# Attention with a routed expert layer: q, k and v remainders of two head pairs in one operation, and the last keys' unit ahead of the first bank

## The chip, the cores and the metric

The kernel runs on one core of a Trainium2 chip. The core has TensorE (PE, matrix products into PSUM), VectorE (DVE), ScalarE (ACT) and GpSimd (POOL) for elementwise work, and DMA queues, most of which are started here by SyncE (SP). Each engine takes its instructions in the order in which the program issued them, and waits where data is not there yet. The metric is the time of one launch on the device, in microseconds (us). The profile is one further execution, taken by the hardware profiler; its span is the stretch from its first instruction to its last.

## The reference

```
cum = np.cumsum(np.maximum(s, 0.0), axis=-1)
bias = -(cum[:, :, :, None] - cum[:, :, None, :])
scores = np.where(causal, -1000000000.0, q @ k.T / 8 + np.minimum(bias, 0.0))
attn = softmax(scores) ; x = attn @ v          # 8 batches, 8 heads, 576 positions, width 64
logits = x @ w_gate                            # 4608 tokens of width 512, 8 experts
...                                            # (token, expert) pairs in order of their logit, 576 tokens for each expert
out[mask] = np.maximum(x[mask] @ w1[e], 0.0) @ w2[e]
```

Causal attention with a bias that falls with a running sum, then a layer of eight experts of which each token gets one. The choice depends on the order of all logits, so the kernel keeps about float32 accuracy: it splits float32 values into a 16-bit part and a 16-bit remainder and multiplies both.

## The kernel before, in words

The change touches attention alone. Attention runs over 16 **groups** g of four heads: two pairs of heads (`pr` 0 and 1), each of two heads (`par` 0 and 1). An order written by hand (`run`, line 600) cuts each group into 14 **units**, seven for each pair of heads. In each unit it issues one unit of scores of the group, then what was posted for that unit, then what the plan `T` puts there for other groups: loads, splits, the maxima, the products with v of scores made seven units earlier.

- **Split of q, k and v** (`prep_units` line 212, `vprep_units` line 271). A raw tile holds both pairs of heads, 2 x 576 elements a partition. `hi2` (line 262) writes the 16-bit part on ACT; `lo2` (line 265) the remainder, x times scale minus the 16-bit part, on DVE, one operation for each pair of heads: for q, k and v six operations of 128x576 a group, all on line 267. After each, `pop` runs a queued small DVE step (denominators). The plan's entries `LO=(2, 3, 5, 7)` and `VLO=(13, 11)` give the units, counted from the start of the split. The split of q and k is made three groups ahead; five copies on SP (`b1a` to `b3`) then bring the parts to their partitions.
- **Maxima** (`spass_units`, line 284). PE makes scores into PSUM and DVE takes their maxima (line 297). `m1` (line 343) scales the nine maxima on POOL in three small steps (lines 350 to 352). They come back to Q through a transpose and two small DMAs (`m2`, `m3`).
- **Scores** (`st_units`, line 374). For each pair of heads there are six **banks** of 512 columns (three for each `par`), and one unit `last` of 128 columns for the last 64 keys. `fin` (line 389) writes P = exp(scores) in float32 on ACT (line 391) and posts the **remainder R** = P minus its upper 16 bits (line 393) three units later: bank (0, 0) and `last` on DVE, the other five on POOL. The entry `RD=((0, 0),)` names the banks whose R is on DVE. For the very last group it is `RE`, in which bank (0, 0) of the second pair of heads is not named, so that it goes to POOL there.
- **Products with v** (`pv_units`, line 438). PE multiplies P's upper half with v and its remainder, and R with v (lines 457 to 459), from the seventh unit on behind the scores. The banks' columns of P and R follow the 128 columns of `last` (`P0 = 128`). The tile of the last 64 queries is the one that needs `last`.
- Around it POOL also writes the remainder of the result (line 496), and SP the result and its transposes to be used for the logits.

After attention the router sorts and assigns the tokens, and the experts run with weights that POOL gathers.

Of the kernel before, what the change touches and what calls it, by code (L numbers as in the profile page):

```python
# [8 lines left out]
F32 = mybir.dt.float32  # L9
F16 = mybir.dt.float16  # L10
BF = mybir.dt.bfloat16
I32 = mybir.dt.int32
AF = mybir.ActivationFunctionType
OP = mybir.AluOpType
# [13 lines left out]
YS = 8.0 * QS * QS  # L28
# [7 lines left out]
LA = 2  # L36
GS = 64.0
START = ((None, None, -25, 4), (None, None, -5, 7), (-13, 0, 10, 6), (3, 7, 21, 5))
T = dict(HI=(0, 1, 2, 2), LO=(2, 3, 5, 7), B=(3, 5, 8, 8, 10), VHI=(6, 8), VLO=(13, 11), RD=((0, 0),), RT=(3, 3),
         XH=(23, 27, 24), XL=(26, 29, 34), XT=(27, 29, 30, 30, 36), LG=(33, 34, 38, 43, 45), M=(2, 5, 10), G=(-50,  # L40
         -42, -26), V=(-17, -14), PV=(7, 7), NT=(1, 1), NA=(1, 1, 1, 0), RE=(((0, 0),
         (0, 2), (1, 1)), ((0, 1),)), NE=(0, 0, 0, 0), RP=1, RQ=204, TL=((16, 23), (16, 23)))
# [4 lines left out]
P0 = 128  # L47
PW = 1536
# [3 lines left out]
def strided_hi(ap):  # L52
    return ap.bitcast(BF).rearrange("p (c two) -> p c two", two=2)[:, :, 1]


class Attention:
# [155 lines left out]
    def prep_units(self, g):  # L212
# [8 lines left out]
        def b1a(odd=True, x="qk"):  # L221
            if odd:
                if "q" in x:
                    d(q_(0, 0, 1), q_(64, 1, 0))
                if "k" in x:
                    d(K[0:64, 0, 1], K[64:128, 1, 1])
            else:
                d(q_(0, 0, 0), q_(0, 1, 0))
                d(K[0:64, 0, 0], K[0:64, 1, 1])
# [20 lines left out]
        if g < 2:  # L250
            b0 = [lambda o=o, x=x: nc.scalar.activation(o, x[0:64], AF.Copy, scale=QS)
                  for o, x in ((q_(0, 0, 0), q), (K[0:64, 0, 0], k))]
            if g:
# [4 lines left out]
            return hi, lo, b0, b1a, b1b, b2, b3  # L258
        return (list(zip(T["HI"], hi)) + list(zip(T["LO"], lo)) +
                list(zip(T["B"], (lambda: b1a(False), b1a, b3, b1b, b2))))  # L260

# [1 line left out]
        return [lambda p=p: self.nc.scalar.activation(o[:, p], x[:, p], AF.Copy, scale=sc) for p in range(2)]  # L263

    def lo2(self, x, h, o, sc):
        def f(p):
            self.nc.vector.scalar_tensor_tensor(o[:, p], x[:, p], sc, h[:, p], op0=OP.mult, op1=OP.subtract)  # L267
            self.pop()
        return [lambda p=p: f(p) for p in range(2)]

    def vprep_units(self, g):
        st = self.st[g]
# [3 lines left out]
        return ([(0, lambda: self.nc.gpsimd.memset(V[:, :, :, 64:65], 1.0))] +  # L276
                list(zip(T["VHI"], self.hi2(st["rv"], V[:, :, :, 0:64], VS))) +
                list(zip(T["VLO"], self.lo2(st["rv"], V[:, :, :, 0:64], Vl, VS))))

# [94 lines left out]
    def st_units(self, g):  # L374

        nc, st = self.nc, self.st[g]
        Q, K = st["Q"], st["K"]
        units = []

        def mm(ps, c0, n, par, pr, ki, q0, diag=False):  # L380
            ks = slice(128 * ki, 128 * ki + 128)
            nc.tensor.matmul(ps[:, c0:c0 + n], K[0:70, 0, par, pr, ks], Q[0:70, 0, pr, par, q0:q0 + n],  # L382
                             start=True, stop=False)
            nc.tensor.matmul(ps[:, c0:c0 + n], K[:, 1, par, pr, ks], Q[:, 1, pr, par, q0:q0 + n],  # L384
                             start=False, stop=not diag)
            if diag:
                nc.tensor.matmul(ps[:, c0:c0 + 128], self.identb, self.mT, start=False, stop=True)

        def fin(ps, pr, c0, n, gp):
            P, R = st["P", pr], st["R", pr]  # L390
            nc.scalar.activation(P[:, c0:c0 + n], ps[:, :n], AF.Exp, scale=1.0 / YS)  # L391
            eng = nc.gpsimd if gp else nc.vector
            self.post(lambda: eng.tensor_tensor(R[:, c0:c0 + n], P[:, c0:c0 + n], strided_hi(P)[:, c0:c0 + n],  # L393
                                                op=OP.subtract), T["RT"][0 if gp else 1])

        def bank(pr, par, j):
            if par == 0 and j == 0:
                st["P", pr] = self.w.tile([128, P0 + 2 * PW], F32, name="P")
                st["R", pr] = self.w.tile([128, P0 + 2 * PW], F16, name="R")
            ps = self.ps_t.tile([128, 512], F32, name="pst")  # L400
            o, t = 64 * par, 0 if par else 512
            if j == 0:
                mm(ps, 0, 512, par, pr, 0, o, diag=True)
            elif j == 1:
                mm(ps, 0, 64, par, pr, 0, t)
                for ki, c0, n in ((1, 64, 384),):
                    mm(ps, c0, n, par, pr, ki, o + 128, diag=True)
                mm(ps, 448, 64, par, pr, 1, t)
            else:
                mm(ps, 0, 256, par, pr, 2, o + 256, diag=True)  # L410
                mm(ps, 256, 64, par, pr, 2, t)
                mm(ps, 320, 64, par, pr, 3, t)
                mm(ps, 384, 128, par, pr, 3, o + 384, diag=True)
            fin(ps, pr, P0 + par * PW + 512 * j, 512, (par, j) not in
                (T["RE"][pr] if g == 2 * self.nb - 1 else T["RD"]))

        def last(pr):


            ps = self.ps_t.tile([128, 512], F32, name="pst")  # L420
            nc.tensor.matmul(ps[:, 0:128], self.identb, self.mL, start=True, stop=False)
            for par in range(2):
                q0 = self.q0(par, 4)
                for a, n in ((0, 70), (1, 128)):
                    k0 = (2 * par + pr) * S + 512 - 64 * par
                    nc.tensor.matmul(ps[:, 64 * par:64 * par + 64],
                                     K[0:n, a].rearrange("p h r s -> p (h r s)")[:, k0:k0 + 128],
                                     Q[0:n, a, pr, par, q0:q0 + 64], start=False, stop=(par == a == 1))
            fin(ps, pr, 0, 128, False)

        for pr in range(2):
            for par in range(2):
                for j in range(3):
                    units.append(lambda pr=pr, par=par, j=j: bank(pr, par, j))
            units.append(lambda pr=pr: last(pr))
        return units

    def pv_units(self, g, pr):
# [980 lines left out]
```

## Time and profile before

| what | us |
|---|---|
| median of 3 runs (859.68 to 864.87) | 862.95 |
| the profiled execution, its own time | 858.84 |
| its span | 857.1 |
| attention in it, to about | 336 |
| a group of attention in the middle (14 units) | 18.65 |
| PE, DVE, ACT, POOL busy over the span | 761.5, 613.0, 387.0, 478.4 |

How to read it: the shares over the span mix two parts. Up to about 336 us the core works on attention, after it on the router and the experts, which the change does not touch. Numbers of the whole page therefore say little of the change; the rows by stage do. The profile names an operation by its line, its engine and its tiles (out<-in), so `R<-P` is the remainder of the exponentials on line 393, on POOL or on DVE. The granted clock of TensorE over the span is 0.942 of full speed, and 1.00 in most of attention. A duration includes the time in which an operation that was issued could not get on.

### The profile page before, as it was taken

How to read it: one execution, taken by the hardware profiler on the slowest of the kernel's cores; microseconds unless marked ns; L12 is line 12 of the kernel's file. 1: busy time of each engine (PE TensorE's matmuls, PEld its weight loads, DVE VectorE, ACT ScalarE, POOL GpSimd, SP SyncE). 2: the span in 40 equal slices, each digit the busy share in tenths (PEclk: the TensorE clock that was granted, in tenths of full speed). 3: DMA queues.
4: the chain of work that ended last, by engine and by line, in shares of the span. 5: the costliest groups of instructions: out<-in, count | busy, mean ns of one | idle time of the engine just before them, and what ended most of it. 6: DMA issues, size and time to landing. Idle time of an engine off the chain costs nothing.

```text
span 857.1 us, 22612 instructions
## 1 busy us (share of the span) xinstructions
PE 761.5 (89%) x9241; PEld 482.7 (56%) x9241; DVE 613.0 (72%) x1578; ACT 387.0 (45%) x866; POOL 478.4 (56%) x587
## 2 busy tenths in 40 slices
PE   8887899989889998269989999998989969959996
PEld 3576777877777787147545455454444525424442
DVE  6789999999999978668768878776677737115110
ACT  5466778878768787024213333231232113214110
POOL 5577899999989996062353534633462342432101
PEclk9689999999999999589999999999998979969999
DMA  6865999898988806052393837546283290491001
GB/s 176 249 178 151 198 238 236 207 236 234 232 205 223 177 31 141 33 187 67 114 188 103 223 101 194 151 134 169 81 211 107 95 221 28 125 210 62 31 13 43
DMA packets 122222, 128.69 MB, mean 150 GB/s; under 512 B 79781, under 2 KB 88329, under 8 KB 122118
## 3 DMA queue, kind: packets, MB, share of 16 engines
q1 hardware_dynamic: 103938, 74.31, 37.1%
q0 software_dynamic: 15744, 52.46, 20.3%
q8 instruction: 72, 1.18, 0.6%
q10 hardware_dynamic: 2436, 0.48, 0.3%
q14 instruction: 32, 0.26, 0.1%
HBM read 71.99 MB, written 19.49 MB: 107 GB/s over the span
## 4 chain that ended last, share of the span: by engine, by line
PE 48%; DVE 24%; issue 12%; DMA 5%; POOL 5%; ACT 3%; another core or an unknown queue 1%; ACTq 0%; SPq 0%; POOLq 0%; DVEq 0%
PE py L1146 15%; PE ph L1109 15%; DVE mr L297 7%; DVE R L393 3%; PE pht L1113 2%; PE py L1137 2%; DVE K L267 2%; DVE Vl L267 2%; PE ph L1111 2%; PE cnt L883 2%; POOL R L393 2%; PE pi L1013 1%; DVE Q L267 1%; DMA md<-mt 1%; DMA Q<-Q 1%
## 5 line engine op out<-in xcount | busy, mean ns | idle before, releaser
L393 POOL TENSOR_TENSOR R<-P 128x512 f16<-128x512 f32 x158 | 195.9, 1254 | 19.3 <-ACT P L391 19.3
L1109 PE MATMUL ph<-xT,w1p 128*128 128x512 f16 x696 | 187.1, 391 | 11.8 <-issue 11.7
L1146 PE MATMUL py<-w2p,hT 128*128 128x512 f16 x768 | 177.1, 381 | 0.3 <-issue 0.3
L1051 POOL DMA_INDIRECT wst<-in_w_dram,iw x96 | 98.3, 1024 | 138.8 <-DVE iw L857 40.4
L1113 PE MATMUL pht<-xT,w1p 128*128 128x64 f16 x768 | 139.0, 195 | 8.9 <-issue 8.7
L297 DVE TENSOR_REDUCE mr<-pss 128x1 f32<-128x512 f32 (+4 forms) x224 | 133.5, 608 | 9.9 <-PE pss L305 5.7
L391 ACT ACTIVATE P<-pst 128x512 f32<-128x512 f32 (+1 forms) x224 | 120.5, 563 | 41.4 <-PE pst L384 14.6
L1158 POOL DMA_INDIRECT out_dram<-y,ids x40 | 42.7, 1068 | 155.9 <-ACT y L1148 127.2
L1109 PEld LDWEIGHTS <-w1p 128*128 128x128 f16 x696 | 69.5, 100 | 93.8 <-issue 22.5
L1146 PEld LDWEIGHTS <-hT 128*128 128x128 f16 x768 | 70.2, 98 | 81.5 <-issue 5.4
L1117 ACT ACTIVATE hT<-ph 128x512 f16<-128x512 f32 x64 | 38.1, 597 | 169.5 <-PE ph L1109 89.0
L459 PE MATMUL po<-V,R 128*128 128x65 f16 x960 | 112.9, 195 | 1.3 <-POOL R L393 1.0
L457 PE MATMUL po<-V,P 128*128 128x65 f16 x960 | 112.4, 196 | 0.9 <-DVE xf L479 0.9
L458 PE MATMUL po<-Vl,P 128*128 128x64 f16 x960 | 112.3, 194 | 0.0
L382 PE MATMUL pst<-Q,K 70*128 70x64 f16 (+4 forms) x512 | 104.7, 253 | 4.3 <-ACT P L391 3.0
L384 PE MATMUL pst<-Q,K 128*128 128x64 f16 (+4 forms) x512 | 105.4, 253 | 0.0
L1126 DVE SCALAR_TENSOR_TENSOR hT<-ph,hT 128x512 f16<-128x512 f32 x64 | 43.8, 687 | 84.9 <-ACT hT L1117 54.4
L457 PEld LDWEIGHTS <-P 128*128 128x128 bf16 x960 | 91.1, 99 | 5.6 <-issue 0.2
L303 PE MATMUL pss<-K,Q 67*128 67x512 f16 (+3 forms) x256 | 72.5, 311 | 22.8 <-DVE mr L297 19.6
L459 PEld LDWEIGHTS <-R 128*128 128x128 f16 x960 | 90.3, 98 | 1.8 <-POOL R L393 1.5
L458 PEld LDWEIGHTS <-P 128*128 128x128 bf16 x960 | 90.2, 100 | 1.1 <-issue 1.0
L1113 PEld LDWEIGHTS <-w1p 128*128 128x128 f16 x768 | 71.3, 99 | 12.9 <-issue 12.2
(223 smaller groups left out, 1562.7 us busy)
## 6 DMA issues: line engine op xcount, KB each, us to landing
rq<-in_q_dram SPq DMA_DIRECT2D x32, 288.0 KB
rk<-in_k_dram SPq DMA_DIRECT2D x32, 288.0 KB
rv<-in_v_dram SPq DMA_DIRECT2D x32, 288.0 KB
Q<-Q SPq DMA_DIRECT2D x62, 144.0 KB
K<-K SPq DMA_DIRECT2D x62, 144.0 KB
xs<-xp SPq DMA_DIRECT2D x32, 256.0 KB
wst<-in_w_dram,iw POOLq DMA_INDIRECT x96
xs<-xp SPq DMA_DIRECT2D x8, 128.0 KB
```

Source lines behind the costliest of these rows:

```text
L297: nc.vector.tensor_reduce(o, ps, AX.X, OP.max)
L382: nc.tensor.matmul(ps[:, c0:c0 + n], K[0:70, 0, par, pr, ks], Q[0:70, 0, pr, par, q0:q0 + n], start=True, stop=False)
L384: nc.tensor.matmul(ps[:, c0:c0 + n], K[:, 1, par, pr, ks], Q[:, 1, pr, par, q0:q0 + n], start=False, stop=not diag)
L391: nc.scalar.activation(P[:, c0:c0 + n], ps[:, :n], AF.Exp, scale=1.0 / YS)
L393: self.post(lambda: eng.tensor_tensor(R[:, c0:c0 + n], P[:, c0:c0 + n], strided_hi(P)[:, c0:c0 + n], op=OP.subtract), T["RT"][0 if gp else 1])
L457: nc.tensor.matmul(po[:, i, :], H[:, c:c + 128], V[:, pr, sl, :], start=f, stop=False)
L458: nc.tensor.matmul(po[:, i, 0:64], H[:, c:c + 128], Vl[:, pr, sl, :], start=False, stop=False)
L459: nc.tensor.matmul(po[:, i, :], R[:, c:c + 128], V[:, pr, sl, :], start=False, stop=l)
L1051: nc.gpsimd.indirect_dma_start(out=t, out_offset=None, in_=src, in_offset=bass.IndirectOffsetOnAxis(ap=iw[:, k:k + 1], axis=0))
L1109: nc.tensor.matmul(ph, w, xT[:, 0:4, 4 * b + c], start=first, stop=last)
L1113: nc.tensor.matmul(pt[:, f], w, xT[:, 4, 4 * b + c, 0:64], start=first, stop=last)
L1146: nc.tensor.matmul(py, hT[:, f, a, 128 * i:128 * i + n], w2p[:, f, b], start=first, stop=last)
```

## The change

1. `lo2` issues one operation over both pairs of heads (128x1152) in place of two of 128x576, for q, k and v. `pop` runs once behind it. The plan's entries become `LO=(3, 7)` and `VLO=(13,)`: the units at which the later halves of q and k stood, and that of the first half of v, whose second half stood two units ahead of it.
2. The unit `last` comes first of the seven units of a pair of heads; the banks follow, each one unit later than before. The tiles P and R are taken in `last`.
3. The remainder R of `last` and of bank (0, 0) is one DVE operation over 640 columns, posted by bank (0, 0) with the same delay of three units; so it stands at unit 4 of the seven, where R of bank (0, 0) stood at unit 3 and that of `last` at unit 9. In the very last group this puts bank (0, 0) of the second pair of heads on DVE too.

```diff
-T = dict(HI=(0, 1, 2, 2), LO=(2, 3, 5, 7), B=(3, 5, 8, 8, 10), VHI=(6, 8), VLO=(13, 11), RD=((0, 0),), RT=(3, 3),
+T = dict(HI=(0, 1, 2, 2), LO=(3, 7), B=(3, 5, 8, 8, 10), VHI=(6, 8), VLO=(13,), RD=(), RT=(3, 3),
...
     def lo2(self, x, h, o, sc):
-        def f(p):
-            self.nc.vector.scalar_tensor_tensor(o[:, p], x[:, p], sc, h[:, p], op0=OP.mult, op1=OP.subtract)
+        def f():
+            self.nc.vector.scalar_tensor_tensor(o, x, sc, h, op0=OP.mult, op1=OP.subtract)
             self.pop()
-        return [lambda p=p: f(p) for p in range(2)]
+        return [f]
...
-        def fin(ps, pr, c0, n, gp):
+        def rest(pr, c0, n, gp):
             P, R = st["P", pr], st["R", pr]
-            nc.scalar.activation(P[:, c0:c0 + n], ps[:, :n], AF.Exp, scale=1.0 / YS)
             eng = nc.gpsimd if gp else nc.vector
             self.post(lambda: eng.tensor_tensor(R[:, c0:c0 + n], P[:, c0:c0 + n], strided_hi(P)[:, c0:c0 + n],
                                                 op=OP.subtract), T["RT"][0 if gp else 1])
 
+        def fin(ps, pr, c0, n, gp):
+            nc.scalar.activation(st["P", pr][:, c0:c0 + n], ps[:, :n], AF.Exp, scale=1.0 / YS)
+            if gp is not None:
+                rest(pr, c0, n, gp)
...
-            fin(ps, pr, P0 + par * PW + 512 * j, 512, (par, j) not in
+            fin(ps, pr, P0 + par * PW + 512 * j, 512, None if par == j == 0 else (par, j) not in
                 (T["RE"][pr] if g == 2 * self.nb - 1 else T["RD"]))
+            if par == j == 0:
+                rest(pr, 0, P0 + 512, False)
...
-            fin(ps, pr, 0, 128, False)
+            st["P", pr] = self.w.tile([128, P0 + 2 * PW], F32, name="P")
+            st["R", pr] = self.w.tile([128, P0 + 2 * PW], F16, name="R")
+            fin(ps, pr, 0, 128, None)
 
         for pr in range(2):
+            units.append(lambda pr=pr: last(pr))
             for par in range(2):
                 for j in range(3):
                     units.append(lambda pr=pr, par=par, j=j: bank(pr, par, j))
-            units.append(lambda pr=pr: last(pr))
         return units
```

More of the change, by code (lines that the diff above doesn't have):

```diff
@@ L394, in fin @@
                                                 op=OP.subtract), T["RT"][0 if gp else 1])
+        def fin(ps, pr, c0, n, gp):
+            nc.scalar.activation(st["P", pr][:, c0:c0 + n], ps[:, :n], AF.Exp, scale=1.0 / YS)
+            if gp is not None:
+                rest(pr, c0, n, gp)
         def bank(pr, par, j):
-            if par == 0 and j == 0:
-                st["P", pr] = self.w.tile([128, P0 + 2 * PW], F32, name="P")
-                st["R", pr] = self.w.tile([128, P0 + 2 * PW], F16, name="R")
             ps = self.ps_t.tile([128, 512], F32, name="pst")
```

## The prediction, made before the changed kernel was run

> **What bounds the kernel now.** I read the page first, then the stretches of attention by engine, then the waits in its middle. The stretches (columns: stretch, its length, then busy time and count for PE, PEld, DVE, ACT, POOL, then granted clock, DMA share, GB/s):
>
> ```profile
> 0.00:95.00 95.00, 80.66 (x944) 55.48 (x945) 76.94 (x148) 54.90 (x121) 61.57 (x119) 0.87 0.68 192
> 95.00:112.00 17.00, 15.60 (x290) 12.75 (x289) 16.73 (x31) 14.09 (x40) 16.68 (x18) 1.00 0.99 213
> ...
> 158.10:176.70 18.60, 17.84 (x354) 14.77 (x351) 18.46 (x38) 15.32 (x42) 18.13 (x21) 1.00 0.85 223
> 176.70:195.40 18.70, 16.85 (x323) 13.86 (x320) 18.56 (x37) 14.29 (x40) 18.23 (x21) 1.00 0.99 228
> ...
> 233.00:273.00 40.00, 36.42 (x675) 29.87 (x672) 38.67 (x84) 30.35 (x81) 35.04 (x41) 0.96 0.91 230
> 273.00:307.00 34.00, 33.24 (x656) 27.75 (x654) 31.32 (x69) 26.52 (x74) 32.73 (x39) 1.00 0.66 148
> 307.00:336.00 29.00, 26.91 (x629) 23.51 (x625) 21.36 (x39) 23.95 (x67) 28.48 (x27) 1.00 0.45 89
> 336.00:857.10 521.10, 456.24 (x3910) 240.45 (x3906) 307.91 (x980) 138.62 (x224) 186.20 (x217) 0.93 0.45 120
> ```
>
> The reader is to see that the last 521 us hold nothing of the change, and that in the middle groups (18.65 us each) two engines are full at once: DVE 18.46 of 18.60 and POOL 18.13. The waits from 112 to 233 us (who waited for whom, us in total, times, longest):
>
> ```profile
> PE pss L303 <- DVE mr L297: 8.5, 13, 1.5
> ...
> POOL R L393 <- ACT P L391: 0.3, 1, 0.3
> ```
>
> PE waits for DVE's maxima, and POOL for nothing: its next input is always there. But "busy" holds waits within an operation. The timeline of POOL, and that of DVE in the same microseconds (start, duration):
>
> ```profile
> 172.42 1.55 POOL L393 TENSOR_TENSOR R<-P 128x512 f16<-128x512 f32 x1
> ...
> 173.98 1.04 POOL L393 TENSOR_TENSOR R<-P 128x512 f16<-128x512 f32 x1
> 174.98 1.21 POOL L496 TENSOR_TENSOR xp<-xf,xp 128x512 f16<-128x512 f32 x1
> 176.15 1.55 POOL L393 TENSOR_TENSOR R<-P 128x512 f16<-128x512 f32 x1
> ```
> ```profile
> 171.59 1.48 DVE L267 SCALAR_TENSOR_TENSOR Vl<-rv,V 128x576 f16<-128x576 f32 x1
> ...
> 174.31 0.85 DVE L393 TENSOR_TENSOR R<-P 128x128 f16<-128x128 f32 x1
> ...
> 175.69 1.11 DVE L267 SCALAR_TENSOR_TENSOR Q<-rq,Q 128x576 f16<-128x576 f32 x1
> 176.72 1.52 DVE L393 TENSOR_TENSOR R<-P 128x512 f16<-128x512 f32 x1
> ```
>
> The same remainder takes POOL 1.04 or 1.55. It takes 1.55 where a DVE operation with two SBUF inputs ends inside it, and that DVE operation is long because it first sat until POOL's operation before it had ended: the one of 128 columns took 0.85, ending at 175.16 behind POOL's end at 175.02. The two take turns at something that only one can hold. So both engines are full of waits for each other. How much, from 139.4 to 214 us, four periods of 18.65 (count | busy us, mean ns), POOL then DVE:
>
> ```profile
> L393 POOL TENSOR_TENSOR R<-P 128x512 f16<-128x512 f32 x41 | 51.4, 1269 | 0.0
> L496 POOL TENSOR_TENSOR xp<-xf,xp 128x512 f16<-128x512 f32 x8 | 11.5, 1442 | 0.0
> L496 POOL TENSOR_TENSOR xp<-xf,xp 128x256 f16<-128x256 f32 x4 | 4.7, 1183 | 0.0
> L350 POOL TENSOR_SCALAR mr<-mr 128x9 f32<-128x9 f32 x8 | 4.6, 575 | 0.7
> ```
> ```profile
> L267 DVE SCALAR_TENSOR_TENSOR Vl<-rv,V 128x576 f16<-128x576 f32 x8 | 10.1, 1261 | 0.0
> L393 DVE TENSOR_TENSOR R<-P 128x512 f16<-128x512 f32 x8 | 9.8, 1223 | 0.0
> L267 DVE SCALAR_TENSOR_TENSOR K<-rk,K 128x576 f16<-128x576 f32 x8 | 9.3, 1161 | 0.0
> L267 DVE SCALAR_TENSOR_TENSOR Q<-rq,Q 128x576 f16<-128x576 f32 x9 | 8.5, 947 | 0.0
> ...
> L393 DVE TENSOR_TENSOR R<-P 128x128 f16<-128x128 f32 x8 | 4.5, 565 | 0.0
> ```
>
> The same operations alone: the lines' shortest (min/median/max ns), the split of the weights in the expert stage, and POOL's other two steps late in attention:
>
> ```profile
> L267 DVE SCALAR_TENSOR_TENSOR Vl<-rv,V x32: 747/1034/1589, 28.0 to 316.4; 128x576 f16<-128x576 f32 x32
> L267 DVE SCALAR_TENSOR_TENSOR Q<-rq,Q x30: 739/756/1367, 11.0 to 275.2; 128x576 f16<-128x576 f32 x30
> L267 DVE SCALAR_TENSOR_TENSOR K<-rk,K x30: 739/926/1527, 12.4 to 279.6; 128x576 f16<-128x576 f32 x30
> ```
> ```profile
> L393 POOL TENSOR_TENSOR R<-P x41: 1032/1165/1607, 138.8 to 213.5; 128x512 f16<-128x512 f32 x41
> L393 DVE TENSOR_TENSOR R<-P x16: 275/888/1525, 139.4 to 211.7; 128x512 f16<-128x512 f32 x8, 128x128 f16<-128x128 f32 x8
> ```
> ```profile
> L1059 DVE SCALAR_TENSOR_TENSOR w1p<-wst,w1p 128x512 f16<-128x512 f32 x56 | 37.2, 684 | 0.5 <-ACT w1p L1055 0.5
> ```
> ```profile
> 309.89 0.25 POOL L350 TENSOR_SCALAR mr<-mr 128x9 f32<-128x9 f32 x1
> ...
> 312.65 0.72 POOL L496 TENSOR_TENSOR xp<-xf,xp 128x256 f16<-128x256 f32 x1
> ```
>
> Waits of a group on POOL: ten remainders at 1269 - 1032 = 2.37 us, two xp of 512 at 1442 - 1210 = 0.46, one of 256 at 1183 - 720 = 0.46, two L350 at 575 - 250 = 0.65: **3.95 us**. On DVE (two of each): (1261 - 747 + 1161 - 739 + 947 - 739 + 1223 - 684 + 565 - 275) x 2 = **3.95 us** too, the shortest of each taken as its own time, 684 from the weights' split, of the same width as the 512 columns, and 1210 for POOL's xp from the row at 174.98. POOL then has 14.7 us of its own in 18.65. Since it is never without input, a group cannot be shorter than those 14.7 plus what DVE's operations block; DVE has 13.9 us without its waits, so it is the one that could go faster. PE, at most 17.84 with its waits in, is next.
>
> **The change, part by part.** The sum is made on the profiled execution: span 857.1, its time 858.84 (1.74 us around the span), which is 4.1 under the median of the three runs, 862.95. I add the differences to the median.
>
> *Merged splits.* A group has three operations of 128x1152 for six of 128x576. One element more costs (684 - 275) / 384 = 1.065 ns, so 1152 take 739 + 613 = 1.35 us alone, and a pair saves 0.13 of DVE's own time.
>
> *Merged remainders.* Two of 640 columns for two of 512 and two of 128: 684 + 136 = 0.82 alone, against 0.96. DVE's own time falls by 6.37 - 5.7 = 0.67 a group, and with five turns instead of ten its waits, at the present mean of 0.395, fall by 2.0: 2.65 us in all.
>
> *What POOL pays*, which decides. An operation of 576 blocks a remainder for 1.55 - 1.03 = 0.52, less than its 0.74 alone: POOL's own start hides the first 0.22. No row shows one of 1152. From below it is the whole saving of a fixed part, blocking two thirds as now; from above it blocks for its whole 1.35. I take 0.52 plus the 613 ns of further elements, 1.13, since the 0.22 is hidden once a turn: 3.4 for three. R of 512 now falls on L350 and costs POOL 0.32; with 128 columns more 0.46, or 0.6 where it meets a remainder: 0.9 to 1.2 for two. R of 128 is almost free now (behind the one at 174.31 POOL's xp started at 174.98 as if nothing stood in its way, and the next remainder 1.17 after it). So POOL's waits become 4.3 (to 4.6) instead of 3.95: **+0.35 a group**, 0.65 at the upper end and -0.67 (the hold itself) at the lower. Half of the turns are gone, and with them half of the hidden starts.
>
> *By stretch.* From 95 to 233 us POOL is full: 138 / 18.65 = 7.4 groups x 0.35 = +2.6. From 233 to 273 router steps on DVE join and POOL has 35.04 of 40.00, so DVE's relief counts, down to two periods of 19.0, 2.0 us; I take -1.5 (0 at the other end: the burst still stands in a row on DVE). From 273 to 307 one group with q and k is left: +0.4. From 307 to 336 POOL is full again (28.48 of 29.00) and loses one remainder, 1.03, as bank (0, 0) of the last pair goes to DVE, whose 640 columns block it for 0.5 more: -0.5. From 0 to 95 POOL is not full (61.57) and the chain runs through DVE's splits and the maxima's small DMAs:
>
> ```profile
> 57.24 1.79 DMA md<-mt
> ...
> 60.45 0.76 DVE Q L267
> ...
> 64.28 1.32 DVE K L267
> ```
>
> Three groups with five merges of 0.14 are 2.1 at most; but maxima behind a merged split wait up to 0.6 longer: -1.0 (from +0.6 to -2.1). Sum: +2.6 - 1.5 + 0.4 - 0.5 - 1.0 = **0.0**.
>
> *At nothing:* the exponentials, matmuls and DMAs are as many as before. `last` ahead of the banks puts each bank's R one unit, 1.33 us, later to POOL, and PE asks for it at the same unit: hidden as long as PE does not wait for R, which no row of 112 to 233 shows; if gone, up to 1.3 once, since POOL then sets the pace anyway. The SP copies of k's remainder wait for the whole of k at unit 7, 0.6 us longer; behind them in SP's queue stand the other copies, the loads and the result's writes, all of groups far ahead or behind: three groups of cover for the copies. `pop` runs 19 instead of 22 times a group for nine steps.
>
> **The rivals.** *The hold is the whole operation.* If POOL stands for all of a DVE operation's own time, merging takes 0.67 a group from it. For: waits on both sides add to the same 3.95. Against: 0.52 for a 0.74 operation. It gives -0.67 x 8.4 = -5.6, -2.2 in the router stretch, -1.0 and -0.8 at the ends: 853.5. The Trainium skill ("SBUF — State Buffer", "SBUF: two separate sides") states this as a rule: GpSimd and a DVE operation with two SBUF inputs hold a port pair as an exclusive lock for the whole instruction, and the loser fully blocks. The rows above agree that there is a lock and that both sides wait; they show less than the whole instruction on POOL's side.
>
> *DVE is what bounds.* For: PE's waits of 8.5 us are for DVE. Against: POOL waits for no input. Groups would go to PE's (17.84 + 16.85) / 2 = 17.35: -1.3 x 8.4 = -10.9, with the rest -3.5: 848.5.
>
> *Slower: long holds in a row.* The split of q at unit 3 and the 640 columns at unit 4 follow each other. If the 640 columns no longer fall on L350 but on remainders, at 0.65 a group (+5.5 in 8.4), and PE, which now asks for R one unit sooner after POOL gets it, stands at its products with v and brings no relief at the router and the start (0), the time is 862.95 + 5.5 - 0.5 + 1.3 = 869. It decides once POOL's lag behind the exponentials exceeds what is left of the slack.
>
> **How the numbers follow.** My forecast, no change that can be measured (0.5%, 4.3 us, is about what a measurement of this kernel tells from none): chance 0.50, 863.0, with its own range 859 to 867 (terms +1.5 to +5, 0 to -2, 0.6 to -2.1). Whole hold 0.17, DVE bound 0.10, slower 0.23. So faster 0.27, same 0.50, slower 0.23. The range leaves out DVE bound and the slower case's far part: 853.5 to 870.
>
> **What would show it.** Right: in the middle DVE busy falls to about 16 of a period of 19.0 while POOL stays full; POOL's remainders come as 1.03 and about 2.15; PE's waits turn from DVE's maxima to POOL's R. A period of 18 or under, or POOL with gaps before R, refutes POOL as the bound. Remainders of 2.4 would show the whole hold. If L393 on DVE stays at 1.2 with POOL's L350 at 0.25, the 640 columns meet remainders. The prediction is wrong if the start gains or loses more than 3 us, which no row bounds well.

## The result, and the profile after

| | before | after |
|---|---|---|
| median, us (4 runs each, on the same chip) | 863.65 | 875.8 |
| ratio, 95% interval | | 1.0144 (1.0114 to 1.0174) |
| profiled execution, its span | 857.1 | 875.5 |

The change makes the kernel 12 us slower. The two profiled executions lie 18.4 us apart, more than the medians, so the stretches below are to be read for their place and not for their last microsecond.

Where it comes from is read off the products of v with R (`po<-V,R`), 60 for each of the 16 groups. The time at which a group's last product starts, from the two traces:

| groups | before, us | after, us | difference | forecast for the stretch | second pair |
|---|---|---|---|---|---|
| first to third | to 105.6 | to 112.0 | **+6.4** | -1.0 | +3.3 |
| fourth to tenth | 131.9 | 133.3 | +1.4 | +2.6 | +2.4 |
| eleventh (the router's first steps) | 21.0 | 26.5 | **+5.5** | -1.5 | +2.7 |
| the last five | 79.5 | 81.6 | +2.1 | -0.1 | +1.6 |
| behind that, to the end of the span | 519.1 | 522.1 | +3.0 | 0 | +4.5 |

The last column is the same difference between two more profiles of these two kernels, `c_after` and `c_before` below: every stretch of attention is longer there too, but the two large differences are only half as large.

The stretches of after by engine (columns as in the prediction). The first four have the edges shown for before, the last one is the eleventh group:

```profile
0.00:95.00 95.00, 76.86 (x855) 52.30 (x856) 69.91 (x120) 51.60 (x114) 57.39 (x113) 0.87 0.63 180
...
158.10:176.70 18.60, 17.38 (x349) 14.35 (x346) 16.32 (x33) 15.30 (x40) 18.12 (x20) 1.00 0.89 233
176.70:195.40 18.70, 16.46 (x313) 13.46 (x312) 16.43 (x30) 15.05 (x40) 18.23 (x21) 1.00 0.93 229
...
233.00:273.00 40.00, 32.29 (x572) 26.24 (x569) 34.73 (x64) 26.75 (x71) 32.69 (x38) 0.91 0.87 214
...
245.30:271.80 26.50, 20.02 (x320) 15.90 (x317) 23.32 (x41) 15.58 (x41) 19.43 (x24) 0.87 0.85 220
```

The middle looks as forecast: DVE fell from 18.46 to 16.32 of 18.60, and POOL stayed full at 18.12. The other two stretches don't: from 0 to 95 us every engine did less work in the same time (PE 855 matmuls instead of 944), so something made all of them wait, and the router's stretch has PE busy for 32.29 of 40.00 instead of 36.42. The same group in before took 21.00:

```profile
237.50:258.50 21.00, 18.40 (x322) 15.02 (x319) 19.94 (x46) 14.62 (x40) 17.82 (x22) 0.92 0.87 214
```

A fixed stretch holds less work where the kernel is late. The tenth group, in before and then in after, gives with the eleventh above what DVE did in the two together: 19.96 + 19.94 = 39.90 us in before and 16.90 + 23.32 = 40.22 in after. It was not relieved here at all.

```profile
217.40:237.50 20.10, 17.95 (x361) 14.90 (x358) 19.96 (x41) 15.98 (x45) 19.37 (x22) 1.00 0.96 235
```
```profile
226.30:245.30 19.00, 17.77 (x359) 14.74 (x356) 16.90 (x33) 15.19 (x41) 18.52 (x21) 1.00 0.85 214
```

What PE waits for in the middle of after, 112 to 233 us (us in total, times, longest):

```profile
PEld L465 <- POOL R L392: 5.6, 5, 1.5
...
PE po L465 <- POOL R L392: 5.0, 5, 1.4
PE pss L303 <- DVE mr L297: 4.4, 6, 0.8
```

In before there was no wait for R at all and 8.5 us for DVE's maxima. Lines stand a few lower in after: R is on line 392, the product with it on 465. POOL, then DVE, by shape, from 139.4 to 214 us (count | busy us, mean ns), and the shortest, median and longest of R:

```profile
L392 POOL TENSOR_TENSOR R<-P 128x512 f16<-128x512 f32 x40 | 54.6, 1381 | 0.0
L502 POOL TENSOR_TENSOR xp<-xf,xp 128x512 f16<-128x512 f32 x8 | 9.3, 1158 | 0.0
L350 POOL TENSOR_SCALAR mr<-mr 128x9 f32<-128x9 f32 x8 | 5.7, 707 | 0.7
L502 POOL TENSOR_TENSOR xp<-xf,xp 128x256 f16<-128x256 f32 x4 | 2.7, 679 | 0.0
```
```profile
L392 DVE TENSOR_TENSOR R<-P 128x640 f16<-128x640 f32 x8 | 11.0, 1372 | 0.0
...
L267 DVE SCALAR_TENSOR_TENSOR Vl<-rv,V 128x1152 f16<-128x1152 f32 x4 | 7.9, 1979 | 0.0
L267 DVE SCALAR_TENSOR_TENSOR Q<-rq,Q 128x1152 f16<-128x1152 f32 x4 | 5.9, 1465 | 0.0
...
L267 DVE SCALAR_TENSOR_TENSOR K<-rk,K 128x1152 f16<-128x1152 f32 x4 | 5.4, 1348 | 0.0
```
```profile
L392 POOL TENSOR_TENSOR R<-P x40: 1036/1041/2235, 140.0 to 214.0; 128x512 f16<-128x512 f32 x40
```

A split of 1152 takes 1.348 alone, and a POOL remainder that meets one takes up to 2.235, that is 1.20 more than 1.036. The Trainium skill ("SBUF — State Buffer", "SBUF: two separate sides") has the loser of the port pair blocked for the whole instruction. Here it was blocked for 1.20 of 1.35, and for 0.52 of 0.74 in before: the whole less 0.15 here and less 0.22 there. POOL's waits in a group are ten remainders at 1381 - 1036 = 3.45 us and two L350 at 707 - 250 = 0.91, together 4.4; the xp steps have none left.

The start. DVE's timeline at the split of q for the fourth group, in before and then in after:

```profile
44.52 1.53 DVE L393 TENSOR_TENSOR R<-P 128x512 f16<-128x512 f32 x1
48.53 0.76 DVE L267 SCALAR_TENSOR_TENSOR Q<-rq,Q 128x576 f16<-128x576 f32 x1 [2.48 <-ACT Q L263]
...
49.51 1.12 DVE L297 TENSOR_REDUCE mr<-pss 128x1 f32<-128x512 f32 x2
```
```profile
49.72 1.36 DVE L267 SCALAR_TENSOR_TENSOR Q<-rq,Q 128x1152 f16<-128x1152 f32 x1 [5.64 <-ACT Q L263]
...
51.07 1.59 DVE L392 TENSOR_TENSOR R<-P 128x640 f16<-128x640 f32 x1
...
52.68 1.64 DVE L297 TENSOR_REDUCE mr<-pss 128x1 f32<-128x512 f32 x3
```

DVE works in order, and its split of q waits for ACT's half. In before, R of the first bank ran inside that wait. In after the scores of that bank come one unit later, its R stands behind the split in DVE's queue, the wait grows from 2.48 to 5.64 us of idle time, and R then stands ahead of the maxima, for which PE waits: they begin 3.17 us later, of which 1.19 is the later split, 0.60 its length, and the rest, 1.38, R (1.59 long). The 1.19 is within the scatter: the split starts at 48.53, 50.15 and 51.50 in three profiles with the code of before up to there (before, `c_before`, `r_before`). The distance from the split to the maxima does not scatter: 0.98 us in each of these three, 1.58 with the splits merged and the old order (`e1`), 2.23 with the order alone (`e2`), 2.96 in after and `c_after`. The other splits of q up to 95 us show it too: 2.25, 2.26 and 2.25 in `e3`, which has them apart behind the new order, for 0.67, 0.68 and 0.76 in `c_before`.

### The profile page after: what moved, and what is told of

Its sections match the earlier page's. It is cut to its first block, busy times and chain, and to the rows that moved or that the text cites. A ratio compares the mean times of both kernels' runs of the same rounds, so it can differ in the third digit from the quotient of the medians.

```text
span 875.5 us, 22549 instructions
## 1 busy us (share of the span) xinstructions
PE 767.8 (88%) x9241; PEld 486.2 (56%) x9241; DVE 588.6 (67%) x1501; ACT 389.0 (44%) x866; POOL 480.7 (55%) x586
## 3 DMA queue, kind: packets, MB, share of 16 engines
q0 software_dynamic: 15744, 52.46, 20.2%
## 4 chain that ended last, share of the span: by engine, by line
PE 46%; POOL 18%; DVE 13%; issue 11%; DMA 5%; ACT 3%; another core or an unknown queue 2%; SPq 1%; ACTq 0%; POOLq 0%; DVEq 0%
PE py L1152 14%; PE ph L1115 13%; POOL R L392 11%; POOL xp L502 3%; PE pht L1119 2%; PE py L1143 2%; DVE mr L297 2%; PE ph L1117 2%; PE cnt L889 2%; PE pi L1019 1%; DVE R L392 1%; DMA md<-mt 1%; DVE ge L876 1%; PE pss L303 1%
## 5 line engine op out<-in xcount | busy, mean ns | idle before, releaser
L392 POOL TENSOR_TENSOR R<-P 128x512 f16<-128x512 f32 x157 | 202.0, 1303 | 24.0 <-ACT P L396 19.7
L297 DVE TENSOR_REDUCE mr<-pss 128x1 f32<-128x512 f32 (+4 forms) x224 | 131.6, 612 | 40.2 <-PE pss L305 29.1
L465 PE MATMUL po<-V,R 128*128 128x65 f16 x960 | 114.7, 196 | 9.3 <-POOL R L392 9.3
L303 PE MATMUL pss<-K,Q 67*128 67x512 f16 (+3 forms) x256 | 73.1, 312 | 22.3 <-DVE mr L297 17.9
```

The lines of the kernel that those rows point to most:

```text
L297: nc.vector.tensor_reduce(o, ps, AX.X, OP.max)
L465: nc.tensor.matmul(po[:, i, :], R[:, c:c + 128], V[:, pr, sl, :], start=False, stop=l)
```

## Experiments

Runs `c_`, `e` and `r_` were made where before takes 810 to 811 us: the part behind the last product with R takes 465.5 us there (`c_before`) instead of 519.1, attention about as long as above (340.7 us instead of 338.0). In the other profiles of `c_`, `e` and `r_` that part takes 465.4 to 480.1 us, though the edits lie in attention, so the 3.0 and 4.5 us that the two pairs differ by there are within its scatter. One per cent is 8.1 us there, and 8.6 in the runs `m_`. Ratios are to before on the same chip, with their 95% interval.

| run | ratio | interval |
|---|---|---|
| c_after | 1.0167 | 1.0129 to 1.0205 |
| e1_splits_only | 1.0095 | 1.0040 to 1.0151 |
| e2_order_only | 1.0148 | 1.0111 to 1.0185 |
| e3_order_and_remainder | 1.0104 | 1.0068 to 1.0140 |
| e4_after_one_more_r_on_dve | 1.0242 | 1.0204 to 1.0281 |
| e5_after_r_one_unit_earlier | 1.0207 | 1.0177 to 1.0237 |
| e6_splits_two_pops | 1.0101 | 1.0036 to 1.0167 |
| e7_order_remainder_r_earlier | 1.0151 | 1.0105 to 1.0197 |
| e8_after_scores_one_unit_earlier | 1.0075 | 1.0042 to 1.0108 |
| e10_order_remainder_scores_earlier | 1.0010 | 0.9974 to 1.0046 |
| e13_order_mended_v_split_merged | 1.0052 | 1.0011 to 1.0094 |
| r_before_router_in_one_batch | 0.9941 | 0.9889 to 0.9992 |
| r_e1_splits_router_in_one_batch | 1.0004 | 0.9960 to 1.0049 |
| r_e8_all_scores_earlier_router_in_one_batch | 1.0052 | 1.0003 to 1.0101 |
| m_before_transpose_one_unit_later | 1.0021 | 1.0000 to 1.0042 |
| m_e1_splits_transpose_one_unit_later | 1.0066 | 1.0049 to 1.0084 |
| m_e8_all_scores_earlier_transpose_later | 1.0062 | 1.0031 to 1.0092 |

### One part alone

`e1` takes the merged splits alone, `e2` the order alone, `e3` the order and the merged remainder, with the splits apart.

```diff
 # e1, against before: lo2 as in the change, and
+LO=(3, 7), VLO=(13,)
 # e2, against before: P and R taken in last, and
         for pr in range(2):
+            units.append(lambda pr=pr: last(pr))
             for par in range(2):
...
-            units.append(lambda pr=pr: last(pr))
 # e3, against after: lo2 as before, and
+LO=(2, 3, 5, 7), VLO=(13, 11)
```

> Only the splits of q, k and v are merged; the order of units and the remainders stay as before. Theory S (the loss comes from the splits: at the start a merged split waits for the ACT halves of both pairs of heads, and DVE's maxima stand behind it): most of the 12 us comes back here, 870 to 876. Theory O (the loss comes from the order of the units): no loss here, 858 to 865. Theory L (long holds block POOL): middle periods of 18.9 to 19.2 instead of 18.65, 866 to 870.

> Only the unit of the last keys comes first; its remainder and that of the first bank stay two operations, and the splits are as before. Theory O (each bank's exponential and remainder comes one unit later while PE asks for it at the same unit): 869 to 876, with PE waiting for R. Theory S: 862 to 865, no change. Theory L: no change either, as the turns at the lock are the same.

> The order and the merged remainder, the splits as before. Theory O: 869 to 876, as much as the order alone. Theory S: 860 to 864, a little gained by two turns fewer a group. If this is the whole loss and the order alone is not, the merged remainder costs it.

The order alone costs 1.5%, as much as the whole change; the remainder merged on top of it takes nothing away or a little (1.0104 for 1.0148, with intervals that overlap); and the splits alone cost 1%. So there are two losses, and the edit that the prediction put at nothing is by the medians the larger. Alone they add up to more than the whole (1.0167). In the trace of `e2` the third group ends 5.5 us later than in `c_before`; in `e1` nothing is lost up to there (-0.1), and 5.4 at the end of attention, nearly all of it in the tenth and eleventh groups (+2.1, +2.8).

The order alone did not do what was expected of it, though. From 112 to 240 us PE never waits for R in `e2`, and still its attention is 12.5 us longer than in `c_before`. What grew is PE's wait for DVE's maxima, in `c_before` and then in `e2`; DVE's rows at the start of `e2` follow:

```profile
PE pss L303 <- DVE mr L297: 8.3, 13, 1.5
```
```profile
PE pss L303 <- DVE mr L297: 11.5, 14, 1.4
```
```profile
50.43 0.76 DVE L267 SCALAR_TENSOR_TENSOR Q<-rq,Q 128x576 f16<-128x576 f32 x1 [3.84 <-ACT Q L263]
...
51.18 1.46 DVE L393 TENSOR_TENSOR R<-P 128x512 f16<-128x512 f32 x1
...
52.66 1.11 DVE L297 TENSOR_REDUCE mr<-pss 128x1 f32<-128x512 f32 x2
```

### Is POOL the bound that costs it?

If POOL's lag alone made the loss, one more remainder on DVE would help. `e4` gives it bank (0, 1).

```diff
-RD=(),
+RD=((0, 1),),
```

> The changed kernel with the remainder of bank (0, 1) on DVE too, two of ten moved off POOL in each group. If POOL is what bounds the middle groups (now 18.7 us with DVE at 16.4 busy), POOL loses 2 x (1.03 - 0.46) and a period falls to 17.5 to 18.0; eight groups give 6 to 9 us, 867 to 870. If the middle is bound by the order of units or PE, the period stays at 18.5 or more and the time at 875.

It is the slowest of all. The stretch of its middle from 139.4 to 214 us:

```profile
139.40:214.00 74.60, 68.12 (x1281) 55.74 (x1278) 67.92 (x127) 58.85 (x155) 60.64 (x70) 0.98 0.90 217
```

POOL has 60.64 of 74.60 and DVE 67.92: neither is full, and a period takes 19.3 us. DVE now has another two-input operation in its row, and PE waits 9.9 us for the maxima behind it (112 to 240 us). So POOL's busy time does not set the pace here. The waits fit latency, the place of an operation in DVE's queue; no run moves that alone.

### Putting the order right, in two ways

`e5` posts DVE's remainder one unit earlier, so that it stands ahead of the split of q again; `e7` does it with the splits apart. `e8` and `e10` issue all scores one unit earlier, so that the banks are where they were in before and `last` stands ahead of them; `e8` is the whole change with this, `e10` has the splits apart. `c_before` (one run, 807.96 us) and `c_after` are the two kernels themselves beside them.

```diff
 # e5, against after; e7, against e3
-RT=(3, 3)
+RT=(3, 2)
 # e8, against after; e10, against e3
-            g, u = divmod(n, 14)
+            g, u = divmod(n + 1, 14)
```

> The kernel before again, for its trace on this chip: attention ends at 343 to 348 us, with the first three groups' products with v at about 63, 87 and 106 us.

> The changed kernel again, beside the others on one chip: about 12 us over the kernel before, all of it in attention (its end at 357 to 361 us), 6 us in the first three groups and 5 at the router's steps.

> The changed kernel with the remainder on DVE posted two units behind the first bank instead of three, so that it stands ahead of the split of q on DVE, as before. Theory Q (queue order: in the start the remainder moved behind a split that waits for ACT, which waits for the maxima's DMA; the remainder was hidden in that wait and now is not): 4 to 6 us come back, all in the first three groups, with the third group's products at 107 to 108 us instead of 112. Theory O (every bank later): nothing comes back there, 112.

> Order and merged remainder, two units behind the first bank, the splits apart as before. Theory Q with the splits as the rest of the loss: the start is as before, the middle gains 1 to 2 us by two turns fewer at the lock, the router stretch loses nothing: within 2 us of the kernel before. Theory O: 7 to 10 us over it, as with three units.

> The changed kernel with all units of scores issued one unit earlier against everything else, so that the banks and the 640-column remainder stand at the units at which the banks and the first bank's remainder stood before; only the last keys' units are then ahead of where they were. Theory Q (the loss of the order is that the banks and remainders moved past other work in the engines' queues): the first three groups end within 1 us of the kernel before (after: 3 to 4 us later), PE no longer waits for POOL's R in the middle (after: 5 to 6 us in 128), and only the splits' loss of 4 to 6 us at the router's steps is left: 1.0 to 1.3% becomes 0.3 to 0.8% over the kernel before. Theory M (merged operations are too long for DVE's queue wherever they stand): still 1.2% or more.

> The same one unit earlier, with the merged remainder and with the splits apart as before. Theory Q: no loss is left, and two turns fewer at the lock in a group give a little: 0 to 3 us under the kernel before. Theory M: 4 us or more over it.

`e10` is before again (1.0010), and its third group ends 0.4 us sooner than in `c_before`. The start in `e10`, DVE's timeline:

```profile
46.40 1.66 DVE L392 TENSOR_TENSOR R<-P 128x640 f16<-128x640 f32 x1
49.92 0.76 DVE L267 SCALAR_TENSOR_TENSOR Q<-rq,Q 128x576 f16<-128x576 f32 x1 [1.87 <-ACT Q L263]
...
50.90 1.12 DVE L297 TENSOR_REDUCE mr<-pss 128x1 f32<-128x512 f32 x2
```

The remainder, 640 columns now, is back inside the wait, and the maxima follow the split. Nor does PE wait for POOL's R from 112 to 233 us any more, in `e8` or `e10`.

The two pairs agree: from 1.0104 to 1.0010 with the splits apart, from 1.0167 to 1.0075 with them merged. The order costs 0.9% or **7.5 us** both times, each known to about 4 us either way by the intervals. What is left in `e8`, 5.3 us over `e10`, belongs to the splits. A caveat: the earlier scores were not tried on before itself, so what they might gain there alone is not known.

`e5` and `e7` were a miss. The third group of `e7` ends 1.6 us sooner than in `c_before`, but by the medians both are slower than the kernels that they start from, `e7` by less than its interval. In `e5` the second group ends at 88.8 us, 3.4 sooner than in `c_after`, and the third at 111.4, as in `c_after`: what the earlier R gained is lost again within a group. Moving DVE's R does nothing for the banks on POOL, which still get theirs one unit later: PE waits for R 8.6 us in `e5` and 6.7 in `e7` (112 to 240 us; 5.4 in `c_after`). The times of `e7` scatter from 810.8 to 822.8, and its profiled run is among the fastest, so its profile says little of its median.

How firm the start is: the third group ends at 111.4 to 114.0 us, mean 112.8, in the five profiles in which R stands behind the split of q (after, `c_after`, `e2`, `e3`, `e4`), and at 105.6 to 112.2, mean 108.5, in the fifteen others of this table and above, `e5` and `e7` among them. The kernel before alone ranges over 4.5 us there (105.6 to 110.1) with the same code up to there. So 4.3 us is the mean loss of the start, and a single pair of profiles can show it half as large again.

### What the merged splits lose

With `e6`, two queued steps are popped behind a merged split instead of one, since nine steps had lost three of their 22 places.

```diff
             self.pop()
+            self.pop()
         return [f]
```

> The merged splits alone, as in the first experiment, but with two queued small steps run behind each instead of one. Theory P (the loss at the router's steps comes from there being three places fewer a group to run them, so that they spread over more of POOL's full time): the tenth and eleventh groups lose under 2 us instead of 5, the time is within 2 us of the kernel before. Theory M: still 5 us over it.

No gain (1.0101 for 1.0095). The eleventh group is shorter in its trace, 20.2 us for 23.7 in `e1`, but the start is longer, within its scatter.

The eleventh group is where the router's first batch of small steps runs on DVE. In the group as after has it, these steps are long; the same step in after and in before:

```profile
L843 DVE CAST w<-dg 128x20 bf16<-128x20 int32 x1 | 1.0, 1006 | 0.0
```
```profile
L837 DVE CAST w<-dg 128x20 bf16<-128x20 int32 x1 | 0.2, 164 | 0.0
```

So one theory is that the router's steps make the loss. In the `r_` runs that batch is moved to the router's last one, for before, for `e1` and for `e8`.

```diff
-        if self.router and b in (3, self.nb - 2):
-            self.post(lambda: self.rq.extend(self.router.batch_steps(b, 0 if b == 3 else 4)), 2)
+        if self.router and b == self.nb - 2:
+            self.post(lambda: self.rq.extend(self.router.batch_steps(b, 0)), 2)
```

> The kernel before, with the router's two batches of steps (after b = 3 and after the last pair of blocks) done as one batch at the last. Both theories: within 3 us of before either way; the time from the ninth to the eleventh group falls by what the router's steps on DVE and their waits took there, 1 to 3 us, and comes back later.

> The merged splits alone, on the same changed router. Theory 'router steps': within 2 us of r_before_router_in_one_batch, and no loss against it at the ninth to eleventh groups (where e1_splits_only lost 5 us against before). Theory 'long holds': 4 to 6 us slower than r_before_router_in_one_batch, at the same groups or spread over all.

> The whole change with its scores one unit earlier, on the same changed router. Theory 'router steps': within 2 us of r_before_router_in_one_batch. Theory 'long holds': 3 to 6 us slower, as e8_after_scores_one_unit_earlier was against before.

The splits cost 1.0004 - 0.9941, 5 us by the medians, without the router's batch as well. The tenth and eleventh groups of `r_before`, then of `r_e1`:

```profile
221.40:241.10 19.70, 17.87 (x358) 14.81 (x355) 19.56 (x40) 16.31 (x45) 19.23 (x22) 1.00 0.84 225
241.10:258.70 17.60, 16.83 (x322) 13.82 (x319) 17.46 (x35) 14.21 (x37) 17.12 (x20) 1.00 0.98 226
```
```profile
219.90:241.90 22.00, 19.38 (x361) 16.11 (x358) 17.79 (x35) 15.74 (x43) 21.29 (x26) 0.92 0.93 229
241.90:259.70 17.80, 16.74 (x319) 13.73 (x315) 16.76 (x33) 14.64 (x40) 17.32 (x20) 1.00 0.99 241
```

In the eleventh the loss is gone with the router's steps (17.8 for 17.6); in the tenth it stays, 2.3 us, as `e1` lost 2.1 there. What happens in it, in `r_e1` on POOL, on DVE, and the waits from 219.9 to 228:

```profile
220.72 0.25 POOL L350 TENSOR_SCALAR mr<-mr 128x9 f32<-128x9 f32 x1
221.04 0.19 POOL L351 CAST mp<-mr 128x9 f16<-128x9 f32 x1
221.32 1.20 POOL L352 TENSOR_TENSOR mp<-mr,mp 128x9 f16<-128x9 f32 x1
```
```profile
221.10 1.35 DVE L267 SCALAR_TENSOR_TENSOR K<-rk,K 128x1152 f16<-128x1152 f32 x1
```
```profile
PEld L359 <- POOL mp L352: 2.0, 1, 2.0
PE psm L359 <- DVE den L471: 1.7, 1, 1.7
```

The merged split of k starts between two of POOL's three small steps on the maxima. The third, 0.21 us when it is free, ends at 222.52, just behind the split at 222.45. PE's transpose of its result (L359) is next in PE's order and stands still. (The second wait is put down to DVE's denominators, which end at 222.55; PE's load had been waiting for L352 all that time.) In every period of `r_before` from the fourth group to the eleventh the transpose stands 2.0 us or more behind the end of that step, and the three steps take 1.14 together; in `r_e1` they take 0.81, 1.13 or 1.80, with 0.1 to 3.2 us behind them. The loss comes where a long one and no slack fall together. In `r_e8` and `e8` the same meeting stands in the eighth group, 22.3 and 22.4 us long for 19.7 in `c_before`.

The last three runs give the transpose one unit more, from the fifth group on.

```diff
-                at(s1 + w + T["M"][1], self.m2, g, pr)
+                at(s1 + w + T["M"][1] + (g > 3), self.m2, g, pr)
```

> Before, with PE's transpose of the maxima one unit (1.33 us) later from the fifth group on. Control: its slack is 2.0 us or more there, so 1.0 within 0.3%, if the later maxima's DMA still lands in time; if that DMA becomes late, 2 us slower or more.

> The merged splits alone, with the transpose one unit later. Theory 'late maxima' (the loss is PE's wait for POOL's small steps behind a merged split): no group of 22 us is left, no wait of PE for POOL's L352 over 0.5 us, and the time is within 1.5 us of m_before_transpose_one_unit_later (e1_splits_only: 5.4 us of attention lost). Theory 'long holds in any place': still 4 us or more slower than it, in other groups.

> The whole change with its scores one unit earlier, and the transpose one unit later. Theory 'late maxima': within 2 us of m_before_transpose_one_unit_later (e8_after_scores_one_unit_earlier: 1.0075 of before). Theory 'long holds in any place': 4 to 6 us slower, as e8 was.

PE's wait for L352 falls from 2.0 to 0.8 us in `m_e1`, and the splits now cost 1.0066 - 1.0021, 3.9 us, for 7.7 in `e1`. By the medians that is less, but `e1`'s interval reaches from 3.2 to 12.2 us, so it is not shown to be less; and it is not the 1.5 that the theory of the late maxima allowed. The tenth group still takes 21.6 us; the control's grew to 21.2 itself, for a reason that was not followed. So the blocked small step is seen as one of the places, and how much of the time it costs is not shown. What `m_e1` loses to its control in the groups lies in the eleventh, with the router's steps: 23.9 us for 21.2.

### One split alone, on the mended order

`e13` is `e10` with the two operations for v alone made one.

```diff
-                list(zip(T["VLO"], self.lo2(st["rv"], V[:, :, :, 0:64], Vl, VS))))
+                list(zip(T["VLO"], self.lo1(st["rv"], V[:, :, :, 0:64], Vl, VS))))
```

> e10 (order and remainder, scores one unit earlier) with the split of v alone in one operation. If fewer turns at the lock are worth what the busy times say: 0 to 2 us faster than before. If long holds cost more than the turns save: 1 to 3 us slower than before.

1.0052 for 1.0010: one merged split is of no use either, and 3 us slower by the medians, with intervals that overlap. The fewer turns of the splits at the port pay nothing in the time of any run; those of the remainder at most a little (`e3` for `e2`).

Nothing found here beats the kernel before but `r_before`, which has none of the change: the router's two batches in one, 0.6% faster by an interval that just leaves out 1. With seventeen comparisons in the table, one such interval can be chance.

## Why the prediction was wrong

It said no change, 863.0 with 853.5 to 870.0; it became 875.8. By its own steps:

- **"At nothing: `last` ahead of the banks"**, the step that failed. It put the later R at "up to 1.3 once", as long as PE doesn't wait for R. The order cost 7.5 us by both pairs of runs. PE did wait for R, 5 times in the middle of after; but the order costs without that too: alone (`e2`) it lost 12.5 us of attention with no such wait from 112 to 240 us. The reason looked at POOL's queue alone. That R of the first bank also passes the split of q in DVE's own queue, from inside a wait to behind it, was not counted, though the row at 44.52 stands in the trace of before; it puts the maxima 1.3 to 1.6 us later at each of those splits.
- **From 0 to 95 us, -1.0 (+0.6 at worst)**: +6.4 in this pair of profiles, +3.3 in the second, 4.3 in the mean of all. The term counted only the merges of splits. `e1`, which has these alone, lost nothing at the start (-0.1).
- **From 233 to 273 us, -1.5 (0 at worst)**: +5.5 in the eleventh group here, +2.7 in the second pair. "DVE's relief counts" expected DVE to be less busy where the router's steps join. It wasn't: 40.2 us over the tenth and eleventh groups for 39.9 in before. The router's small steps grew by what the merges had saved, as the cast of 1006 ns for 164 shows; that these steps and the late maxima are what PE's lost time comes from is argued, not shown.
- **From 95 to 233 us, +2.6**: near in size, but by luck. The groups of before alternate between 17.5 and 19.8 us, so that an even number has to be averaged: 18.65. In after each takes 19.0 to 19.1, POOL's waits are 4.4 (4.3 to 4.6 forecast), the longest remainder 2.24 (2.15), DVE's share 16.3 (16). But the +0.35 of the merge is not what made the period: the order alone has 19.25 over the same four groups, the fifth's end to the ninth's, and the merged splits alone have 18.8 in `e1` and 18.45 in `r_e1` and `m_e1`, less than before, with POOL as full (18.13 of 18.46). In `e8` the period of 19.2 comes from the one group of 22.4. The merge's price on POOL depends on where the operations meet, and no fixed price a group is shown.
- **Behind 273 us, -0.1**: +2.1 in the last five groups. Most of it goes with the order: they take 81.6 to 82.9 us with it (after, `c_after`, `e2`, `e3`), 80.0 and 80.9 with the scores one unit earlier (`e10`, `e8`), 79.5 and 80.7 in the two profiles of before.
- **The rivals.** DVE as the bound fell: DVE got 2.1 us a group, and the period grew; without the new order it fell by 0.2 (`r_e1`, `m_e1`) or rose by 0.15 (`e1`). The whole hold came nearer in the hold itself (1.20 of 1.35) but not in the time. The slower rival had PE's stand at the products with v, which came, but at 869 it counted no loss at the start and at the router, where 12 of the 15 us of attention were lost in this pair, and 6 of 10 in the second. Its own condition, the 640 columns on remainders instead of L350, isn't what decided: L350 still takes 707 for 250 alone.
- **Its sums.** "DVE has 13.9 us without its waits" does not follow from its rows: 18.46 - 3.95 is 14.5, hardly less than POOL's 14.7, so it was nearly a tie which of the two could go faster. The extremes of its own terms give 860 to 868.5, not 859 to 867. Neither moves the forecast.

What stays open: where the splits' 4 to 8 us go in full, since no run has both the router's batch and the transpose out of the way; and how the order's 7.5 us divide between DVE's queue and the banks that POOL gets one unit later.

## What to carry to other kernels

When a step moves by a unit, write down for each in-order queue what it now stands behind: an operation that ran for nothing inside a wait can cost nearly its whole length once it stands behind the waiting one (1.38 of 1.59 us here). Merging two operations that share a port with another engine saves their fixed part and turns, but lengthens the longest hold (here from 0.74 to 1.35 us), and what can pay for it are the shortest steps that others wait for; ask how much slack stands behind these and whether the pattern ever drifts to none. A stretch in which many short steps share the engine is the last place to count its lower busy time as a gain.

## What was not expected of the hardware

A stop of PE can cost more than its length. The stretch of `r_e1` around the blocked step (granted clock is the third number from the end):

```profile
220.90:222.50 1.60, 0.00 (x0) 0.00 (x0) 1.60 (x4) 0.00 (x0) 1.45 (x4) 1.00 1.23 91
222.50:224.50 2.00, 1.93 (x31) 1.68 (x32) 1.00 (x3) 0.26 (x2) 2.00 (x4) 0.85 1.19 294
224.50:226.50 2.00, 2.00 (x31) 1.88 (x29) 1.95 (x3) 1.69 (x5) 2.00 (x4) 0.50 0.91 279
226.50:228.50 2.00, 2.00 (x28) 1.46 (x26) 1.02 (x4) 1.37 (x3) 2.00 (x2) 0.80 0.95 202
```

PE stands for about 1.7 us, and within two microseconds of its return the granted clock falls to 0.50; it is back at 1.00 by 228.5: 0.15 x 2 + 0.5 x 2 + 0.2 x 2 = 1.7 us of full speed lost on top. The Trainium skill ("TensorE: Matmul & The Clock Gate", "What's actually happening") puts the half rate behind an idle window of about 3.4 us; here a stop of half that length was followed by it. The stop does not always bring it: the same one in `e1` did (0.50 from 225 to 227 us), but in after PE stands for 2.39 us from 246.97 and the granted clock stays at 1.00 up to 261. What decides is not shown by any run here.
